# Where operand tiles start in SBUF: one attention-plus-MLP kernel with its weight blocks, x tiles and g tiles moved by multiples of 16 bytes

## The chip, the cores and the metric

The kernel runs on one core of one Trainium2 chip. The metric is the device time of one execution in microseconds (us). The kernel before has a median of 676.92 us in two runs (676.63 and 677.21).

## What is computed

Sliding-window attention with four sink positions, and then a two-layer MLP over the same tokens. The reference, cut to its core:

```python
# q, k, v: (4, 8, 768, 64); n_sink 4, window 128
scores = q @ k^T / sqrt(64)
keep = is_sink | in_window          # 4 first positions, or the last 128
a = exp(where(keep, scores, -1e9) - max); a = a / (sum(a) + 1e-9)
x = (a @ v) -> (3072, 512)          # heads side by side
h = x @ w_in                        # 512 -> 2048
g = max(h, 0) + alpha * min(h, 0)
out = g @ w_out                     # 2048 -> 512
```

## The kernel before

**Tiling.** The 3072 tokens are worked on in 12 chunks of 256 (`QC`). The 2048 hidden columns are worked on in 16 blocks of 128 (`f` = 0 to 15). For each chunk the attention part makes x, transposed, as four pieces of 128 x 256 (`kt` = 0 to 3). Each pair of chunk and block is one *round* of the MLP.

**Two parts per number.** The weights arrive as 64-bit floats and are turned on the chip into a high and a low 32-bit part. x and g are split likewise (`xh`, `xl`, `gh`, `gl`). Every product is the sum of three: high by high, high by low, low by high.

**One round.** `gemm1` (line 895) runs twelve matmuls of 256 columns into one PSUM bank: for each `kt`, `xh` and then `xl` stream past the high part of the w_in block, and then `xh` past the low part. So x is the moving operand, and a 128 x 128 slice of the weight block is loaded into the array. ScalarE and VectorE then make g (lines 899 and 900) and split it (901 and 902). `gemm2` runs two rounds later (`LAG` = 2) and is six matmuls of 512 columns: here the w_out half of the block is the moving operand and halves of `gh` or `gl` are loaded into the array (lines 932 and 933 with `gh`, line 930 with `gl`). TensorE loads the weights of the next matmul while one is running (rows PEld in the profile), and each of the eighteen matmuls of a round has its own load.

```python
for n, (part, rhs) in enumerate(((0, x1), (0, x2), (1, x1))):
    nc.tensor.matmul(h(), fin.at[:, 0, part, ks], rhs.at[:, kt], ...)   # L895
...
nc.tensor.matmul(o2[j].at, gh.at[:, js], fin.at[:, 1, 0], ...)          # L932
nc.tensor.matmul(o2[j].at, gh.at[:, js], fin.at[:, 1, 1], ...)          # L933
nc.tensor.matmul(o2[j].at, gl.at[:, js], fin.at[:, 1, 0], ...)          # L930
```

**Weights stay in SBUF.** Each block `f` has 8 KB of each partition in the pool `const`, under the tag `w0` to `w15`. The DMA (line 373) lands the raw 64-bit block there, ACT and DVE convert it by way of `wa` (lines 383 to 405), and the result is written over the raw block. This happens once, in about the first 113 us; after that all sixteen blocks lie still and are only read. The blocks 14 and 15 also serve, before their weights arrive, as room for the first heads (`lent`).

**What sets the order.** A planner (`Plan`) draws up one order of all operations before anything is built, from costs written down in the code. It knows of operations and of how many tiles of a kind there are, not of addresses. Each kind of tile (`xh`, `xl`: 2 each; `gh`, `gl`: `LAG + 1` = 3 each) is handed out in turn. Within a chunk the attention of the next chunk is spread over the first twelve rounds; the last chunk has none to carry, so that its sixteen rounds hold matmuls of `gemm1` and `gemm2` and almost nothing else. Since `gemm2` lags by two, the first two `gemm2` of a chunk's rounds are those of blocks 14 and 15 of the chunk before.

**Addresses.** Tiles of a pool lie one behind the other, each starting at a multiple of 32 bytes of the partition. `const` holds, before the weight blocks, only small tiles, and block 14 comes first of the blocks. Counted modulo 128 bytes, the kernel before has its operands here: all weight blocks at 32, but block 14 at 64; `xh` and `xl` at 96; `gh` and `gl` at 32 (a tile of 64 bytes named `gap` ahead of them is used by nothing). The inner slices of all these tiles start at multiples of 512 bytes, so that every slice has the place of its tile.

Of the kernel before, what the change touches and what calls it, by code (L numbers as in the profile page):

```python
# [9 lines left out]
F32 = mybir.dt.float32  # L10
F32R = mybir.dt.float32r
# [4 lines left out]
I32 = mybir.dt.int32  # L16
# [3 lines left out]
P = 128  # L20
B, H, S, D = 4, 8, 768, 64
DM, DF = 512, 2048
NS = 4
WIN = 2 * P + NS
QC = 2 * P
# [4 lines left out]
KT = DM // P  # L30
LAG = 2
# [47 lines left out]
class Plan:  # L79
# [20 lines left out]
    def held(self, tile_):  # L100
        v = Value(None)
        v.at = tile_
        return v

    def op(self, engine, cost, run, reads=(), writes=(), tail=0.09, mode=None, nbytes=0, other=None, locks=False):
        o = Op(engine, cost, tail, run, self.rank if engine == "PE" else None)
        o.ways = {engine: (cost, run)}
        if other:
            o.ways[other[0]] = other[1:]
        o.born = self.rank  # L110
        if engine == "PE":
            self.rank += 1
        o.mode, o.nbytes, o.index = mode, nbytes, len(self.ops)
        seen = []
        for group, writing in ((reads, False), (writes, True)):
            for x in group:
                v, key = x if isinstance(x, tuple) else (x, None)
                if v not in seen:
                    seen.append(v)
                keys = [k for k in set(v.wrote) | set(v.read) if key is None or k is None or k == key]  # L120
                for k in keys:
                    o.before.update(v.wrote.get(k, ()))
                    if writing:
                        o.before.update(v.read.get(k, ()))
                if writing:
                    for k in keys:
                        if key is None or k == key:
                            v.wrote.pop(k, None)
                            v.read.pop(k, None)
                    v.wrote.setdefault(key, []).append(o)  # L130
                else:
                    v.read.setdefault(key, []).append(o)
        for v in seen:
            v.left += 1
        o.values = seen
        o.takes = [v for v in seen if v.kind]
        o.locks = locks
        self.ops.append(o)
        return o
# [144 lines left out]
def dve(n, fast=False):  # L284
    return 0.07 + (0.52e-3 if fast else 1.04e-3) * n


def cast(n, psum=False):
    return (0.045 if psum else 0.092) + 0.84e-3 * n


def act(n, psum=False):
    return (0.153 if psum else 0.135) + 0.84e-3 * n
# [28 lines left out]
def program(ctx, tc, qk, pairs, vp, vq, vs, w, par, out):  # L322
    nc = tc.nc
    const = ctx.enter_context(tc.tile_pool(name="const", bufs=1))
    fast = ctx.enter_context(ExitStack())
    pool = fast.enter_context(tc.tile_pool(name="main", bufs=1))
    psum = ctx.enter_context(tc.tile_pool(name="psum", bufs=1, space=bass.MemoryType.PSUM))
    plan = Plan(tc)
# [6 lines left out]
    def several(name, n, shape, dtype):  # L335
        plan.kind(name, [pool.tile(shape, dtype, name=f"{name}{i}") for i in range(n)])

    scratch = ctx.enter_context(tc.tile_pool(name="scratch", bufs=1, space=bass.MemoryType.DRAM))
    plan.kind("swap", [scratch.tile([4, P, P], F32, name=f"swap{i}") for i in range(2)])
    plan.kind("turns", [scratch.tile([4, P, 2 * 32], F32, name=f"turns{i}") for i in range(2)])  # L340
# [13 lines left out]
    several("sinkT", 1, [P, QC], F32R)  # L354
    several("vs", 1, [P, DM], F32R)
    several("ob", 2, [P, DM], F32)
    several("xh", 2, [P, KT, QC], F32R)
    several("xl", 2, [P, KT, QC], F32R)
    several("g", 2, [P, QC], F32)
    pool.tile([P, 16], F32, name="gap")  # L360
    several("gh", LAG + 1, [P, QC], F32R)
    several("gl", LAG + 1, [P, QC], F32R)

    size = const.tile([P, NF], F32, name="size")
    sizes = held(size)
    raws, fins = {}, {}

    def load_weights(f, engine="ACT"):
        raw = raws[f] = held(None)

        def run():
            raw.at = const.tile([P, 2 * DM, 2], I32, tag=f"w{f}", name="wraw")
            (nc.sync if engine == "SP" else nc.scalar).dma_start(
                raw.at.rearrange("p (i x) w -> p i (x w)", i=2), w[f].bitcast(I32).rearrange("i p x -> p i x"))
        return op(engine, ISSUE if engine == "SP" else 0.12, run, writes=[raw] + lent.get(f, []), nbytes=8 * P * 2 * DM)

    def convert_weights(f):
        raw, fin, wa = raws[f], held(None), val("wa")
        fins[f] = fin
        n = 2 * DM  # L380
        low, high = lambda: raw.at[:, :, 0], lambda: raw.at[:, :, 1]
        wf = lambda: wa.at.bitcast(F32).rearrange("p (i x) -> p i x", i=2)
        first = op("ACT", act(n) + 0.09, lambda: nc.scalar.activation(  # L383
            wa.at.bitcast(F32), high().bitcast(F32), AF.Abs, scale=REBIAS, accum_out=size[:, f:f + 1]),
            reads=[raw], writes=[wa, (sizes, f)])
        if f < LATER:
            op("DVE", dve(n, True), lambda: nc.vector.tensor_scalar(wa.at, wa.at, 3, None, op0=ALU.logical_shift_left), writes=[wa])
            op("DVE", dve(n), lambda: nc.vector.scalar_tensor_tensor(
                wa.at, low(), 29, wa.at, op0=ALU.logical_shift_right, op1=ALU.bitwise_or), reads=[raw], writes=[wa])
        else:  # L390
            three = held(None)
            op("ACT", act(n), lambda: nc.scalar.activation(
                low(), raw.at.bitcast(U16).rearrange("p x (w s) -> p x w s", s=2)[:, :, 0, 1], AF.Copy, scale=2.0 ** -13, bias=-0.5 + 2.0 ** -14),
                reads=[raw], writes=[three])
            op("DVE", dve(n), lambda: nc.vector.scalar_tensor_tensor(  # L395
                wa.at, wa.at, 3, low(), op0=ALU.logical_shift_left, op1=ALU.bitwise_or), reads=[raw, three], writes=[wa])
        op("DVE", dve(n), lambda: nc.vector.scalar_tensor_tensor(  # L397
            wa.at, high(), -0x80000000, wa.at, op0=ALU.bitwise_and, op1=ALU.bitwise_or), reads=[raw], writes=[wa])

        def high_part(engine):  # L400
            fin.at = const.tile([P, 2, 2, DM], F32R, tag=f"w{f}", name=f"w{f}")
            (nc.scalar.copy if engine == "ACT" else nc.vector.tensor_copy)(fin.at[:, :, 0], wf())
        op("ACT", cast(n), lambda: high_part("ACT"), reads=[wa], writes=[(fin, 0), raw],
           other=("DVE", dve(n, True), lambda: high_part("DVE")))
        op("DVE", dve(n), lambda: nc.vector.tensor_tensor(  # L405
            fin.at[:, :, 1], wf(), fin.at[:, :, 0].bitcast(F32), ALU.subtract), reads=[wa, (fin, 0)], writes=[(fin, 1)])
        return first
# [82 lines left out]
    then(lambda: load_head(0, 2))  # L490
    then(lambda: load_head(0, 4))
    then(lambda: load_weights(0, "SP"))
    then(lambda: vs_prep(0))
    then(lambda: load_head(0, 6))
    then(lambda: load_v(0, 0))
    then(lambda: load_v(0, 2))
    for f in range(1, FIRST):
        then(lambda: load_weights(f, "SP"))
        if f == 2:
            then(lambda: load_head(1, 0))  # L500
            then(lambda: load_head(1, 2))
# [36 lines left out]
    for i, m in ((0, P), (1, P), (1, 0), (2, P), (2, 0)):  # L538
        o = m + NS if m else m
# [8 lines left out]
    xh, xl, prep, comb, sink, ptile_, sums, rinv, nms, wt = {}, {}, {}, {}, {}, {}, {}, {}, {}, {}  # L548
# [460 lines left out]
    def fetch(upto):  # L1009
        nonlocal nload  # L1010
        while nload < min(NF, upto):
            o = load_weights(nload)
            if nload - AHEAD in begun:
                plan.order_after(o, begun[nload - AHEAD])
            nload += 1
# [89 lines left out]
    with tc.If(bad != 0):  # L1105
# [3 lines left out]
        with tc.For_i(0, B, 1) as b:  # L1109
            for cc in range(CPB):  # L1110
                x = general(nc, gen, ptile, cc, b, qk5, vp5, nsink, window, ident)
# [167 lines left out]
```

## Time and profile before

| what | value |
|---|---|
| median of two runs | 676.92 us |
| span of the profiled execution (first to last instruction) | 674.6 us |
| matmuls / weight loads in the profile | 4534 / 4534 |
| of these in `gemm1` / `gemm2` | 2304 / 1152 in the program |
| VectorE, ScalarE busy | 525.4 us, 397.9 us |
| mean DMA rate | 126 GB/s |

The profiled execution's own span is 674.6 us, 2.3 us under the median of the runs; what lies ahead of the first and behind the last instruction is not in the span.

How to read it: the matmuls overlap in the records, since the end that the profile gives to a matmul is modelled. What a matmul takes of the time of TensorE is the distance from its start to the start of the next one. In a stretch without waits the given duration is that distance plus 0.163 us, so that a mean duration of 282 ns stands for 119 ns from start to start, and one of 390 ns for 227 ns. PEld rows are weight loads, which run beside the matmuls.

### The profile page before, as it was taken

Reading aid. Unit: us, or ns where it says so; the run is one execution under the profiler, and the core shown is the slowest. Engines: PE = TensorE matmul, PEld = TensorE weight load, DVE = VectorE, ACT = ScalarE, POOL = GpSimd, SP = SyncE. Lnnn points to the kernel's source line nnn. Section 1 sums busy time; section 2 is a strip of 40 time slices with the busy share of each in tenths; the row PEclk is TensorE's granted clock in tenths of the full one; section 3 lists DMA queues with packets and bytes.
Section 4 is the critical chain, followed back from the end, with each engine's and each line's share of the span. In section 5 each row is a group of like instructions: output and inputs, shape, how many; then the busy total and the mean of one; then the engine's idle time right before and its main releaser. Section 6 shows DMA issues by size and latency. Waiting matters only on the chain.

```text
span 674.6 us, 13245 instructions
## 1 busy us (share of the span) xinstructions
PE 661.7 (98%) x4534; PEld 579.3 (86%) x4534; DVE 525.4 (78%) x1750; ACT 397.9 (59%) x1066; POOL 35.0 (5%) x115
## 2 busy tenths in 40 slices
PE   9989999999999999999999999999999999999996
PEld 4667898888989989989988988988998988998995
DVE  6999999968967977986986985995995994994331
ACT  5999888827537627736636635744744753853332
POOL 2110000001000000010000000010000000000000
PEclk9999999999999999999999999999999999999999
DMA  8684641424343443443434433542542542420000
GB/s 319 218 307 155 241 162 48 119 76 154 119 126 107 128 143 106 139 136 86 142 117 119 142 118 89 159 141 59 174 129 72 162 131 87 142 94 17 32 2 35
DMA packets 58683, 85.19 MB, mean 126 GB/s; under 512 B 9072, under 2 KB 35056, under 8 KB 58608
## 3 DMA queue, kind: packets, MB, share of 16 engines
q1 hardware_dynamic: 55056, 71.17, 34.5%
q10 hardware_dynamic: 3552, 13.11, 5.3%
q8 instruction: 37, 0.61, 0.4%
q14 instruction: 38, 0.31, 0.2%
HBM read 67.22 MB, written 17.04 MB: 125 GB/s over the span
## 4 chain that ended last, share of the span: by engine, by line
PE 81%; DVE 11%; ACT 5%; issue 2%; POOL 0%; ACTq 0%; POOLq 0%
PE bank L895 35%; PE bank L932 11%; PE bank L933 11%; PE bank L930 11%; PE bank L787 3%; PE bank L599 3%; PE bank L598 3%; DVE wa L397 2%; PE bank L876 2%; DVE w L405 2%; ACT pt L615 1%; DVE wa L395 1%; ACT wa L383 1%; PE bank L1087 1%; DVE g L900 1%
## 5 line engine op out<-in xcount | busy, mean ns | idle before, releaser
L895 PE MATMUL bank<-xh,w 128*128 128x256 f32 x1536 | 307.5, 282 | 0.5 <-DVE g L900 0.3
L895 PEld LDWEIGHTS bank<-xh,w 128*128 128x128 f32 x1536 | 250.0, 189 | 9.3 <-DVE g L900 3.4
L895 PE MATMUL bank<-xl,w 128*128 128x256 f32 x768 | 214.9, 280 | 0.1
L899 ACT ACTIVATE g<-bank,param 128x256 f32<-128x256 f32 x192 | 90.7, 473 | 115.8 <-PE bank L895 110.1
L932 PE MATMUL bank<-w,gh 128*128 128x512 f32 x382 | 150.6, 394 | 0.2
L933 PE MATMUL bank<-w,gh 128*128 128x512 f32 x382 | 149.4, 391 | 0.0
L895 PEld LDWEIGHTS bank<-xl,w 128*128 128x128 f32 x768 | 144.4, 188 | 4.2 <-DVE xl L809 0.3
L615 ACT ACTIVATE pt<-pt,nm 128x260 f32<-128x260 f32 (+1 forms) x192 | 94.5, 493 | 54.0 <-DVE nm L611 53.5
L900 DVE TENSOR_TENSOR g<-bank,g 128x256 f32<-128x256 f32 x192 | 79.7, 419 | 50.7 <-ACT g L899 49.5
L930 PE MATMUL bank<-w,gl 128*128 128x512 f32 x382 | 118.9, 392 | 0.0
L901 ACT CAST gh<-g 128x256 fp32r<-128x256 f32 x192 | 76.9, 404 | 60.9 <-DVE g L900 60.7
L902 DVE TENSOR_TENSOR gl<-g,gh 128x256 fp32r<-128x256 f32 x192 | 80.4, 423 | 26.4 <-ACT gh L901 23.0
L611 DVE CUSTOM_DVE_ANT_0 pt<-bank,masks 128x260 f32<-128x260 f32 (+1 forms) x192 | 74.9, 400 | 19.4 <-PE bank L599 15.8
L930 PEld LDWEIGHTS bank<-w,gl 128*128 128x128 f32 x382 | 70.6, 188 | 14.9 <-issue 0.7
L932 PEld LDWEIGHTS bank<-w,gh 128*128 128x128 f32 x382 | 71.7, 188 | 9.7 <-ACT gh L901 1.0
L933 PEld LDWEIGHTS bank<-w,gh 128*128 128x128 f32 x382 | 71.8, 188 | 8.1
L564 DVE TENSOR_TENSOR kq<-stage,kq 64x392 fp32r<-64x392 f32 x80 | 45.3, 567 | 2.7
L660 POOL TENSOR_TENSOR sink<-pt,ri 128x8 f32<-128x8 f32 x80 | 20.8, 263 | 503.9 <-DVE ri L645 386.1
L598 PE MATMUL bank<-kq 128*128 128x260 f32 (+1 forms) x160 | 44.5, 278 | 1.3 <-DVE nm L611 1.2
L599 PE MATMUL bank<-kq 128*128 128x260 f32 (+1 forms) x160 | 45.1, 282 | 0.0
L656 DVE CUSTOM_DVE_ANT_0 comb<-pt,ri 128x128 f32<-128x128 f32 x136 | 43.1, 343 | 0.4
L562 ACT CAST kq<-stage 128x392 fp32r<-128x392 f32 x80 | 40.9, 512 | 0.6 <-PE bank L599 0.2
(130 smaller groups left out, 685.5 us busy)
## 6 DMA issues: line engine op xcount, KB each, us to landing
stage<-qk SPq DMA_DIRECT2D x80, 324.0 KB, 2.9
wraw<-w ACTq DMA_DIRECT2D x12, 1024.0 KB, 5.6
swap<-comb SPq DMA_DIRECT2D x36, 256.0 KB, 2.0
comb<-swap SPq DMA_DIRECT2D x36, 256.0 KB, 3.1
v<-vq SPq DMA_DIRECT2D x36, 192.0 KB, 2.7
out_dram<-ob SPq DMA_DIRECT2D x22, 256.0 KB, 3.6
wraw<-w SPq DMA_DIRECT2D x4, 1024.0 KB, 11.0
v<-vp SPq DMA_DIRECT2D x8, 192.0 KB, 7.3
```

Of the source, the lines that this page charges most:

```text
L598: nc.tensor.matmul(s[:, w0], qh()[:, qs], ks()[:, kw], start=True, stop=False)
L599: nc.tensor.matmul(s[:, w0], ql()[:, qs], ks()[:, kw], start=False, stop=True)
L611: op("DVE", dve(n), lambda: nc.vector.tensor_tensor_reduce(out=pt.at[:, u, w0], in0=s.at[:, w0], in1=masks[:, i, w0], scale=-0.125, scalar ...
L615: op("ACT", exp(n), lambda: nc.scalar.activation(pt.at[:, u, w0], pt.at[:, u, w0], AF.Exp, bias=nm.at[:, h, u:u + 1], scale=-1.0, accum_ou ...
L895: nc.tensor.matmul(h(), fin.at[:, 0, part, ks], rhs.at[:, kt], start=(kt == 0 and n == 0), stop=(kt == KT - 1 and n == 2))
L899: op("ACT", act(QC, True), lambda: nc.scalar.activation(g.at, h(), AF.Copy, scale=alt[:, f:f + 1]), reads=[bk, known("param")], writes=[g])
L900: op("DVE", dve(QC), lambda: nc.vector.tensor_tensor(g.at, h(), g.at, ALU.max), reads=[bk], writes=[g])
L901: op("ACT", cast(QC), lambda: nc.scalar.copy(gh.at, g.at), reads=[g], writes=[gh])
L902: op("DVE", dve(QC), lambda: nc.vector.tensor_tensor(gl.at, g.at, gh.at.bitcast(F32), ALU.subtract), reads=[g, gh], writes=[gl])
L930: nc.tensor.matmul(o2[j].at, gl.at[:, js], fin.at[:, 1, 0], start=False, stop=(f == NF - 1))
L932: nc.tensor.matmul(o2[j].at, gh.at[:, js], fin.at[:, 1, 0], start=(f == 0), stop=False)
L933: nc.tensor.matmul(o2[j].at, gh.at[:, js], fin.at[:, 1, 1], start=False, stop=False)
```

## The change

The instructions, their order, their engines and their waits are the same. What changes is where three groups of tiles start in SBUF:

- Each weight block has 8224 bytes in place of 8192 (`4 * DM + 8` words), so that the start moves on by 32 bytes modulo 128 from one block to the next; and for `f` = 4 to 7 and 12 to 15 the block is used from 16 bytes behind the tile's start.
- `xh0` and `xl0` come first, then a tile of 8 bytes that takes 32, then `xh1` and `xl1`.
- `gh` and `gl` are laid out in three sets, with a tile of 40 bytes (it takes 64) behind each; the former `gap` of 64 bytes is gone.

```diff
+    def apart(name, n, kinds, shape, words):
+        sets = []
+        for i in range(n):
+            sets.append([pool.tile(shape, F32R, name=f"{k}{i}") for k in kinds])
+            pool.tile([P, words], F32, name=f"gap{name}{i}")
+        for k, tiles in zip(kinds, zip(*sets)):
+            plan.kind(k, list(tiles))
...
-    several("xh", 2, [P, KT, QC], F32R)
-    several("xl", 2, [P, KT, QC], F32R)
+    apart("x", 2, ("xh", "xl"), [P, KT, QC], 2)
     several("g", 2, [P, QC], F32)
-    pool.tile([P, 16], F32, name="gap")
-    several("gh", LAG + 1, [P, QC], F32R)
-    several("gl", LAG + 1, [P, QC], F32R)
+    apart("g", LAG + 1, ("gh", "gl"), [P, QC], 10)
...
+    def placed(f, dtype, name):
+        o = f // 4 % 2 * 4
+        return const.tile([P, 4 * DM + 8], dtype, tag=f"w{f}", name=name)[:, o:o + 4 * DM]
...
-            raw.at = const.tile([P, 2 * DM, 2], I32, tag=f"w{f}", name="wraw")
+            raw.at = placed(f, I32, "wraw").rearrange("p (x w) -> p x w", w=2)
...
-            fin.at = const.tile([P, 2, 2, DM], F32R, tag=f"w{f}", name=f"w{f}")
+            fin.at = placed(f, F32R, f"w{f}").rearrange("p (i n x) -> p i n x", i=2, n=2)
```

Where the operands start, in bytes modulo 128, from the addresses that the two programs are built with:

| operand | before | after |
|---|---|---|
| w0 to w3 | 32, 32, 32, 32 | 96, 32, 64, 96 |
| w4 to w7 | 32, 32, 32, 32 | 16, 48, 80, 112 |
| w8 to w11 | 32, 32, 32, 32 | 0, 32, 64, 96 |
| w12 to w15 | 32, 32, 64, 32 | 16, 16, 80, 80 |
| xh0, xl0 / xh1, xl1 | 96 / 96 | 96 / 0 |
| gh0, gl0 / gh1, gl1 / gh2, gl2 | 32 / 32 / 32 | 32 / 96 / 32 |

All other tiles keep their size. Those that lie behind a moved one move along with it by multiples of 32 bytes, the constants `ident`, `param`, `tri` and `masks` among them.

## The prediction

> **What bounds the kernel now.** I read the page's table of engines first, then the chain of work that ended last, then the busy time in three stretches, and then the groups of TensorE inside the long stretch.
>
> ```profile
> PE 661.7 (98%) x4534; PEld 579.3 (86%) x4534; DVE 525.4 (78%) x1750; ACT 397.9 (59%) x1066; POOL 35.0 (5%) x115
> ...
> PE 81%; DVE 11%; ACT 5%; issue 2%; POOL 0%; ACTq 0%; POOLq 0%
> ```
>
> ```profile
> 0.00:115.00 115.00, 109.42 (x704) 83.60 (x704) 106.33 (x243) 97.67 (x219) 11.24 (x34) 1.00 0.59 211
> 115.00:665.00 550.00, 548.45 (x3818) 492.92 (x3817) 418.21 (x1506) 298.39 (x845) 23.72 (x81) 1.00 0.37 110
> 665.00:674.60 9.60, 3.82 (x17) 2.78 (x15) 0.85 (x2) 1.81 (x4) 0.00 (x0) 0.89 0.17 61
> ```
>
> The columns of the stretches are the time, then busy time and count of PE, PEld, DVE, ACT and POOL, the granted clock (1.00 is full; 0.89 in the tail), the DMA share and GB/s. The reader is to see two regimes. Up to 115 us VectorE is full (106.33 of 115) with converting the weights. From 115 to 665 us TensorE is busy 548.45 of 550.00 us at a full clock, with 418.21 us of VectorE beside it. So in 550 of the 674.6 us nothing but the distance from one matmul to the next counts, and a change that adds no instruction can move the time only through that distance (or by making the first stretch longer).
>
> What that distance is now, from the groups of this long stretch (columns: count, busy us, mean ns of one, idle before):
>
> ```profile
> L895 PE MATMUL bank<-xh,w 128*128 128x256 f32 x1343 | 268.3, 282 | 0.5 <-DVE g L900 0.3
> L895 PE MATMUL bank<-xl,w 128*128 128x256 f32 x671 | 187.7, 280 | 0.1
> L932 PE MATMUL bank<-w,gh 128*128 128x512 f32 x336 | 132.1, 393 | 0.0
> L933 PE MATMUL bank<-w,gh 128*128 128x512 f32 x335 | 131.0, 391 | 0.0
> L930 PE MATMUL bank<-w,gl 128*128 128x512 f32 x334 | 103.8, 392 | 0.0
> ```
>
> With 163 ns taken off each modelled duration, `gemm1` has (1343 x 282 + 671 x 280) / 2014 - 163 = 118.3 ns a matmul, 1.42 us a round of twelve; `gemm2` has 392 - 163 = 229 ns, 1.374 us a round of six. The stretch holds 2014 / 12 = 168 rounds. These 168 x 2.79 = 469 us are the bulk of the 550.
>
> **Does the place of a tile show in the trace before?** Once in each chunk it does, since block 14 lies at 64 and the other fifteen at 32. The last chunk carries no attention, so that its rounds can be laid side by side. Its start times, with the first matmul of each part:
>
> ```profile
> 621.35 0.28 PE L895 MATMUL bank<-xh,w 128*128 128x256 f32 x1
> ...
> 622.77 0.40 PE L932 MATMUL bank<-w,gh 128*128 128x512 f32 x1
> ...
> 624.17 0.28 PE L895 MATMUL bank<-xh,w 128*128 128x256 f32 x1
> ...
> 625.54 0.39 PE L932 MATMUL bank<-w,gh 128*128 128x512 f32 x1
> ...
> 626.91 0.28 PE L895 MATMUL bank<-xh,w 128*128 128x256 f32 x1
> ...
> 628.33 0.39 PE L932 MATMUL bank<-w,gh 128*128 128x512 f32 x1
> ...
> 629.69 0.28 PE L895 MATMUL bank<-xh,w 128*128 128x256 f32 x1
> ```
>
> The `gemm2` at 622.77 is that of block 14 (from the chunk before), at 625.54 of block 15, at 628.33 of block 0. They take 624.17 - 622.77 = 1.40, 1.37 and 1.36 us. So `gemm2` with the weight block 32 bytes off the place of `gh` costs 0.04 us more than with both at 32. The same in single matmuls, line 930 of block 14 (first row) and of block 0 (second):
>
> ```profile
> L930 PE MATMUL bank<-w,gl 128*128 128x512 f32 x2 | 0.6, 400 | 0.0
> ```
>
> ```profile
> L930 PE MATMUL bank<-w,gl 128*128 128x512 f32 x2 | 0.6, 389 | 0.0
> ```
>
> `gemm1` reads otherwise. With the same places (x at 96, block at 32) it takes 622.77 - 621.35 = 1.42 us for block 0, 1.37 for block 1 and 1.42 for block 2. So the same places allow two speeds, and what went before picks one. For block 14, at the end of the chunk:
>
> ```profile
> 657.51 0.28 PE L895 MATMUL bank<-xh,w 128*128 128x256 f32 x1
> ...
> 658.92 0.39 PE L932 MATMUL bank<-w,gh 128*128 128x512 f32 x1
> ...
> 660.29 0.28 PE L895 MATMUL bank<-xh,w 128*128 128x256 f32 x1
> ...
> 661.70 0.40 PE L932 MATMUL bank<-w,gh 128*128 128x512 f32 x1
> ```
>
> Block 13 (x and block 64 apart) takes 658.92 - 657.51 = 1.41 us, block 14 (32 apart) 661.70 - 660.29 = 1.41 us. Here the place does nothing.
>
> **The change, part by part.** Nothing is added or removed, no instruction moves in any queue, no wait is new.
>
> *`gemm2`.* Before, block and g stand at the same place in fifteen blocks of sixteen. After, g stands at 32 in two of its three sets and at 96 in one, and the sets go round. Two blocks (1, 9) match the 32 and three (0, 3, 11) the 96, so the two agree in 2/3 x 2/16 + 1/3 x 3/16 = 0.15 of the rounds. Of the 168 rounds 143 then disagree, against the 11 or so of block 14 now: 132 rounds more. The price of one is bounded by the rows above: 0.04 us by the undisturbed neighbours (1.40 against 1.36), and 1.40 - 1.374 = 0.026 us against the mean of all rounds, which pay for other things too. That is 132 x 0.026 = 3.4 to 132 x 0.04 = 5.3 us. A gain at other distances than 32 isn't excluded by any row; it is bounded below by 1.36 us in all rounds, -(1.374 - 1.36) x 168 = -2.4 us. I take 5 us, near the undisturbed pair.
>
> *`gemm1`.* Before, x and block stand 64 apart (32 for block 14); after, 16, 32, 48, 64 and so on, and 0. Nearest row: block 14, no difference. A mixture of places is already there in the attention, where the two `kq` tiles start at 96 and 0 and their slices add 0, 16 and 32 bytes:
>
> ```profile
> L599 PE MATMUL bank<-kq 128*128 128x260 f32 x130 | 36.8, 283 | 0.0
> ```
>
> 283 against the 280 of `xl` above is 3 ns more, of which four more columns are 4 x 117 / 256 = 1.8 ns. The rest, 1.2 ns on 2014 matmuls, is 2.4 us. The other way, if all rounds ran at the quick 1.37 us: 168 x 0.05 = -8.4 us. So -8.4 to +2.4 us; I take 0, since the row that has this very instruction at another place shows none.
>
> *The first stretch.* The conversions on VectorE set its end. They write and read blocks at 32 and, for block 14, at 64 without a difference:
>
> ```profile
> L405 DVE TENSOR_TENSOR w<-wa,w 128x1024 fp32r<-128x1024 f32 x16 | 19.5, 1221 | 0.8 <-ACT w L402 0.8
> ...
> L397 DVE SCALAR_TENSOR_TENSOR wa<-wraw,wa 128x1024 int32<-128x1024 int32 x16 | 19.5, 1216 | 0.1
> ```
>
> ```profile
> L405 DVE TENSOR_TENSOR w<-wa,w x16: 1215/1220/1227, 18.8 to 111.9; 128x1024 fp32r<-128x1024 f32 x16
> ```
>
> Shortest and longest of sixteen are 1215 and 1227 ns: price 0; if each of some 56 such instructions took the 12 ns more, 0.7 us. The loads of blocks 4 to 7 and 12 to 15 land 16 bytes off. The cover is the time from issue to first use, tightest for block 12:
>
> ```profile
> 78.15 0.37 ACTq L373 DMA_DIRECT2D wraw<-w  x1
> ...
> 85.00 1.15 ACT L383 ACTIVATE wa<-wraw 128x1024 f32<-128x1024 f32 x1
> ```
>
> ```profile
> wraw<-w ACTq DMA_DIRECT2D x12, 1024.0 KB, 5.6
> ```
>
> 6.85 us against a median of 5.6 to landing leaves 1.2 us. So a landing that is 20% longer costs nothing; one twice as long would cost 4.4 us here, and what is late next is the conversion on a full VectorE. Price 0.
>
> *Sum:* 5 + 0 + 0 = +5 us. The profiled execution's 674.6 us become 679.6; the runs' median stands 2.3 us above its span, so 676.9 + 5 = 682 us.
>
> **The rivals.** (1) *No effect.* The difference at block 14 comes from something else that returns once a chunk (it is the turn to a new chunk), and the place is read without cost: 677 us. Against it: block 15 has its turn right behind and is back at 1.37. The Trainium skill has this rival as a rule: "TensorE: Matmul & The Clock Gate", section "Step-by-step: what each phase is for", gives the array two independent SBUF read ports, so that loading the next weights takes nothing from the running matmul, and "SBUF — State Buffer", section "Who interferes with whom", says that PE and ACT never wait on anyone. By that rule the sum would be 0 and the time 677 us; the 400 against 389 ns of line 930 speak against it.
>
> (2) *Faster.* The two speeds of `gemm1` at equal places say that a lock between the running matmul and the load beside it decides. Broken by places that change each round, it may fall into the quick one: -8.4 - 2.4 = -10.8 us, 666 us. For it: block 1's 1.37 us came right behind block 14's odd place. Against it: the `gemm2` in front of it had paid 0.04 us, which is nearly all that was won.
>
> (3) *Slower than the forecast.* Most places are as bad as the worst pair seen, 400 against 389 ns, for `gemm2` throughout, and half as much (half the columns) for `gemm1`: 11 x 1008 + 5.5 x 2014 = 22 us, 699 us. It counts as slower, beyond 2% (13.5 us), from about 60% of that price on. Against it: block 14's `gemm1`.
>
> (4) *The loads.* Landings at 16-byte starts take twice as long: some 4 to 9 us of the first stretch, 681 to 686 us without the rest.
>
> **How the numbers follow.** A small loss (677.5 to 690.5 us): 0.53; its likeliest is 682. No effect: 0.12. Faster, 664 to 676: 0.18, of which 0.04 beyond 2%. Worse than 690.5: 0.15. The loads: 0.02, inside the same bounds as the small loss. The range from 668 to 694 leaves out some 0.07 below and 0.12 above. A change of about 2% is what a measurement of this kernel can tell from none; 2% are 663.4 and 690.5 us. So faster 0.04, slower 0.15, same 0.81.
>
> **What would show it.** In the profile after: line 930, 932 and 933 at means of some 395 to 398 ns instead of 391 to 393, line 895 at 280 to 282 still, the same counts, and a first stretch that still ends near 115 us. In the last chunk, `gemm2` at 1.40 us where block and g differ and 1.36 where they agree (block 9). Wrong, if line 895 moves by more than 2 ns in the mean, if the distance of blocks and g doesn't sort the rounds, or if ScalarE's first reads of the raw blocks begin to wait for DMA.

## The result and the profile after

The kernel after takes 682.63 us (median of 2 runs, 682.52 to 682.75) against 676.92 us: a ratio of 1.0085, 95% interval [1.0055, 1.0114]. That is slower, by 5.7 us, and within 2%. The forecast was 682 us. The total came out as forecast, in part by luck: of its two big terms one was too large and the other, put at nothing, was not nothing.

First the page of the kernel after, the table of engines and the loads of the weights, and then the busy time in the two long stretches:

```profile
PE 668.2 (98%) x4534; PEld 584.6 (86%) x4534; DVE 526.7 (77%) x1750; ACT 398.9 (59%) x1066; POOL 34.5 (5%) x115
...
wraw<-w ACTq DMA_DIRECT2D x12, 1024.0 KB, 5.4
```

```profile
0.00:115.00 115.00, 109.59 (x698) 84.83 (x699) 106.24 (x241) 97.11 (x217) 10.64 (x33) 0.99 0.58 211
115.00:665.00 550.00, 548.54 (x3783) 491.33 (x3782) 417.89 (x1505) 298.00 (x843) 23.84 (x82) 1.00 0.36 110
```

The span grew from 674.6 to 680.8 us. The first stretch is as full of VectorE as before (106.24 against 106.33 us) and the twelve loads of ScalarE's queue land as fast (5.4 against 5.6 us). In the same 550 us TensorE got through 3783 matmuls in place of 3818, at a full clock, and as busy as before. Every matmul takes a little longer. By groups of the long stretch:

```profile
L904 PE MATMUL bank<-xh,w 128*128 128x256 f32 x1327 | 268.3, 283 | 0.4 <-DVE g L909 0.2
L904 PE MATMUL bank<-xl,w 128*128 128x256 f32 x664 | 186.6, 281 | 0.1
L941 PE MATMUL bank<-w,gh 128*128 128x512 f32 x330 | 130.5, 395 | 0.0
L942 PE MATMUL bank<-w,gh 128*128 128x512 f32 x330 | 130.2, 394 | 0.0
L939 PE MATMUL bank<-w,gl 128*128 128x512 f32 x331 | 104.1, 395 | 0.0
```

(Line 904 is the former 895, lines 941, 942 and 939 the former 932, 933 and 930.) `gemm2` went up by 2 to 3 ns a matmul, and `gemm1`, which was to stay, by 1 ns. These means are rounded to a nanosecond, which on 3000 matmuls is worth some us; adding up the distances from start to start in both traces, from 115 us to the end, gives it more closely:

```
start to next start, us in all      before    after
gemm1 (xh and xl past w)             238.9    242.7   +3.8
gemm2 (w past gh and gl)             236.0    238.6   +2.6
attention (kq, sinkT, wa, comb)       76.7     76.7    0.0
```

Five more matmuls of `gemm1` fall into this stretch after (2016 against 2011), which is 0.6 of its 3.8 us; so `gemm1` grew by 3.2 and `gemm2` by 2.6 us, together 5.8 us of the 6.2 us of the span, and what is left falls to the first stretch, whose conversions end 0.7 us later (113.8 against 113.1 us; in `e8_w14_in_step` below, which as a whole takes as long as before, they end at 113.6 us).

What the last chunk shows, in starts of the parts (`gemm1` of block 0, `gemm2` of block 14, `gemm1` of block 1, `gemm2` of block 15, and so on, as in the prediction), and further on `gemm2` of block 9:

```profile
626.97 0.28 PE L904 MATMUL bank<-xh,w 128*128 128x256 f32 x1
...
628.39 0.40 PE L941 MATMUL bank<-w,gh 128*128 128x512 f32 x1
...
629.79 0.28 PE L904 MATMUL bank<-xh,w 128*128 128x256 f32 x1
...
631.23 0.40 PE L941 MATMUL bank<-w,gh 128*128 128x512 f32 x1
...
632.64 0.28 PE L904 MATMUL bank<-xh,w 128*128 128x256 f32 x1
...
634.06 0.39 PE L941 MATMUL bank<-w,gh 128*128 128x512 f32 x1
...
635.45 0.28 PE L904 MATMUL bank<-xh,w 128*128 128x256 f32 x1
...
659.52 0.39 PE L941 MATMUL bank<-w,gh 128*128 128x512 f32 x1
...
660.91 0.28 PE L904 MATMUL bank<-xh,w 128*128 128x256 f32 x1
```

`gemm2` takes 1.40, 1.41 and 1.39 us here. Block 9 stands at 32 like its g (both at 160 modulo 256) and was to be back at 1.36; it takes 660.91 - 659.52 = 1.39 us. The three rounds of this chunk whose block and g agree modulo 128 (blocks 1, 9 and 11) take 1.387, 1.387 and 1.399 us by unrounded starts, the others between 1.380 and 1.412: the distance doesn't sort them. `gemm1` takes 1.42, 1.44 and 1.42 us. The rounds are no longer alike, and no `gemm2` of these is as quick as the 1.36 us that was usual before.

### The profile page after: what moved, and what is told of

The parts are those of the page before. It is cut to its first block, busy times and chain, and to the rows that moved or that the text cites. A ratio compares the mean times of both kernels' runs of the same rounds, so it can differ in the third digit from the quotient of the medians.

```text
span 680.8 us, 13245 instructions
## 1 busy us (share of the span) xinstructions
PE 668.2 (98%) x4534; PEld 584.6 (86%) x4534; DVE 526.7 (77%) x1750; ACT 398.9 (59%) x1066; POOL 34.5 (5%) x115
## 4 chain that ended last, share of the span: by engine, by line
PE 88%; DVE 4%; ACT 4%; DMA 1%; issue 1%; POOL 0%; SPq 0%; ACTq 0%; POOLq 0%
PE bank L904 39%; PE bank L941 13%; PE bank L942 12%; PE bank L939 12%; PE bank L796 3%; PE bank L608 3%; PE bank L607 3%; PE bank L885 2%; ACT pt L624 1%; DMA wraw<-w 1%; ACT wa L392 1%; DVE wa L406 1%; PE bank L869 1%; ACT w L411 1%; DVE pt L620 0%
## 5 line engine op out<-in xcount | busy, mean ns | idle before, releaser
L904 PE MATMUL bank<-xh,w 128*128 128x256 f32 x1536 | 312.4, 284 | 0.4 <-DVE g L909 0.2
L908 ACT ACTIVATE g<-bank,param 128x256 f32<-128x256 f32 x192 | 90.7, 473 | 122.6 <-PE bank L904 121.3
## 6 DMA issues: line engine op xcount, KB each, us to landing
wraw<-w SPq DMA_DIRECT2D x4, 1024.0 KB, 11.9
```

What stands on the lines that cost most here:

```text
L908: op("ACT", act(QC, True), lambda: nc.scalar.activation(g.at, h(), AF.Copy, scale=alt[:, f:f + 1]), reads=[bk, known("param")], writes=[g])
```

## The experiments

Two theories were set against each other. *D*: the distance between the two operands of a matmul, the streaming and the loaded one, sets its price, pair by pair. *L*: the train of matmuls and loads falls into a repeating beat when all rounds have the same places, the beat's level depends on the places, and places that change from round to round break it. Times of each run are compared with runs of the kernel before on the same chip (676.8 to 677.0 us).

**One half of the change alone.** `e1_w_only` moves the blocks only, `e2_xg_only` x and g only, to the kernel after's places modulo 128 (the tiles are made 128 bytes longer, so that their places modulo 256 differ from those of the kernel after).

```diff
...
+    WORDS = (16, 0, 8, 16, 28, 4, 12, 20, 24, 0, 8, 16, 28, 28, 4, 12)
+    def placed(f, dtype, name):
+        return const.tile([P, 4 * DM + 32], dtype, tag=f"w{f}", name=name)[:, WORDS[f]:WORDS[f] + 4 * DM]
...
```

```diff
+    def shifted(name, words, n, view, **k):
+        plan.kind(name, [pool.tile([P, n + 32], F32R, name=f"{name}{i}")[:, o:o + n].rearrange(view, **k) for i, o in enumerate(words)])
...
-    several("xh", 2, [P, KT, QC], F32R)
-    several("xl", 2, [P, KT, QC], F32R)
+    shifted("xh", (0, 8), KT * QC, "p (k x) -> p k x", k=KT)
+    shifted("xl", (0, 8), KT * QC, "p (k x) -> p k x", k=KT)
...
-    several("gh", LAG + 1, [P, QC], F32R)
-    several("gl", LAG + 1, [P, QC], F32R)
+    shifted("gh", (0, 16, 0), QC, "p x -> p x")
+    shifted("gl", (0, 16, 0), QC, "p x -> p x")
```

> Only the weight blocks are moved, to the places of the kernel after; x stays at 96, g at 32. Theory D (the distance of the two operands of a matmul sets its price, and only gemm2 pays): 147 of 168 rounds have block and g apart, 136 more than before, at 0.026 to 0.04 us: +3.5 to +5.4 us, 680.5 to 682.5 us, gemm1's mean durations unchanged at 282 and 280 ns, and in the last chunk gemm2 of blocks 1 and 9 back at 1.36 us. Theory L (one relation for all rounds lets the train of matmuls fall into a repeating beat, and places that change from round to round break it, for all matmuls): some +4 to +6 us as well, but gemm1's means go up by 1 to 2 ns, and blocks 1 and 9 cost as much as the others in gemm2, about 1.39 us.

> Only x (96 / 0) and g (32 / 96 / 32) are moved, as in the kernel after; the blocks stay at 32, block 14 at 64. Theory D: a third of the gemm2 rounds, 56, are at a distance of 64, at 0.026 to 0.04 us: +1.5 to +2.2 us, about 679 us; gemm1 as before; in the last chunk two gemm2 of three at 1.36 us and the third at about 1.40. Theory L: x changes once a chunk and g in every third round, so the beat is broken three times less often than with the blocks moved: +1 to +4 us, and the gemm1 that follows an odd gemm2 changes too.

Measured: 682.43 us, ratio 1.0076 [1.0059, 1.0093], and 682.22 us, 1.0074 [1.0057, 1.0091]. Either half costs nearly the whole, so the halves don't add. With the blocks moved, `gemm1` is up as well (283 and 281 ns by the same groups) and `gemm2` of blocks 1 and 9, which stand with their g modulo 256 too, takes 1.38 us, nearer to L's 1.39 than to D's 1.36. With x and g moved, D had 679 us and L at most 4 us more than before; both are passed. All of `gemm2`, not a third, sits at 1.38 to 1.405 us, and from block 2 to block 11 the third whose g is 64 bytes off is the quickest (1.38 us), where D had it as the slowest.

**All blocks at one place.** `e3_w14_as_others` puts all blocks at 32 modulo 128, `e4_all_w_64` all at 64, with blocks 8320 bytes apart in place of 8192 (`WORDS` all 0 but 24 for block 14; or all 8 but 0 for block 14).

> Block 14 is put at 32 like the other fifteen: one relation for the whole kernel. Theory D: 11 rounds win 0.026 to 0.04 us, -0.3 to -0.4 us, 676.5 us. Theory L: the same, and in the last chunk all gemm2 at 1.36 us, block 15's too, and gemm1 at 1.41 to 1.42 throughout, so that block 1's 1.37 us is gone. No effect of places at all: 676.9 us and gemm2 of block 14 still 1.40 us.

> All sixteen blocks at 64, block 14's place, x at 96 and g at 32: one relation again, but 32 bytes apart in gemm2. Theory D: every gemm2 costs what block 14's does, 1.40 us: 157 rounds more at 0.026 to 0.04 us, +4.1 to +6.3 us, 681 to 683 us. Theory L: with one relation the beat holds; its level is that of this relation, equal in all gemm2 of the last chunk to 0.01 us, and may lie on either side of 1.40: 670 to 684 us.

Measured: 678.71 us, 1.0027 [1.0013, 1.004], and 681.85 us, 1.0074 [1.0057, 1.009]. The first was to be a little quicker than before and is slower. A round of its last chunk (`gemm1` of block 4, `gemm2` of block 2):

```profile
634.42 0.28 PE L900 MATMUL bank<-xh,w 128*128 128x256 f32 x1
...
635.83 0.40 PE L937 MATMUL bank<-w,gh 128*128 128x512 f32 x1
...
637.22 0.28 PE L900 MATMUL bank<-xh,w 128*128 128x256 f32 x1
```

`gemm2` takes 1.39 us, not 1.36, though modulo 128 all is as before. What differs is the step of the blocks, 8192 + 128, so that modulo 256 every other block stands 128 bytes off. If 128 bytes were the period that counts, this would change nothing. The same round of `e4_all_w_64`, whose `gemm2` rounds take 1.385 to 1.400 us, near block 14's 1.40:

```profile
636.70 0.28 PE L900 MATMUL bank<-xh,w 128*128 128x256 f32 x1
...
638.11 0.39 PE L937 MATMUL bank<-w,gh 128*128 128x512 f32 x1
...
639.50 0.28 PE L900 MATMUL bank<-xh,w 128*128 128x256 f32 x1
```

**One distance at a time, strides as before.** The next four keep tiles and blocks as long as they were and move whole groups with a pad (in e6 and e7 what lies behind g is put back, modulo 256, by a second one).

```diff
# e5_x_at_0: x 160 bytes on
+    pool.tile([P, 40], F32, name="gapx")
     several("xh", 2, [P, KT, QC], F32R)
...
-    pool.tile([P, 16], F32, name="gap")
+    pool.tile([P, 40], F32, name="gap")
# e6_no_gap: g 64 bytes back
-    pool.tile([P, 16], F32, name="gap")
# e7_g_128_on: g 128 bytes on
-    pool.tile([P, 16], F32, name="gap")
+    pool.tile([P, 48], F32, name="gap")
# e8_w14_in_step: all blocks but 14, x and g 160 bytes on
     idle = const.tile([P, 2], BF16, name="idle")
+    const.tile([P, 40], F32, name="gapw")
```

> Only x is moved, all four tiles by 160 bytes (from 224 to 128 modulo 256), so that x and block are 96 apart in every gemm1 but block 14's; blocks and g stay. Theory D for gemm1 (the distance of x and block sets the level; the runs so far show 119.8 ns a matmul at 96 and 116.1 at 64 or 192): gemm1's means go up by 3 to 4 ns, 2016 x 15/16 x 3.7 = +7 us, 684 us, gemm2 at 229 ns as before. The forecast's step (the place does nothing in gemm1): 677 us. Theory L (only mixing places costs): 677 us, since all rounds are alike, with perhaps another level of the beat.

682.94 us, 1.0075 [1.0047, 1.0104]: the step of the forecast that put `gemm1` at nothing is refuted by moving x alone (g lies 256 bytes further on, at the same place modulo 256). Two rounds in a row, `gemm1`, `gemm2`, `gemm1`, `gemm2`:

```profile
636.96 0.28 PE L896 MATMUL bank<-xh,w 128*128 128x256 f32 x1
...
638.41 0.39 PE L933 MATMUL bank<-w,gh 128*128 128x512 f32 x1
...
639.80 0.28 PE L896 MATMUL bank<-xh,w 128*128 128x256 f32 x1
...
641.23 0.40 PE L933 MATMUL bank<-w,gh 128*128 128x512 f32 x1
...
642.60 0.28 PE L896 MATMUL bank<-xh,w 128*128 128x256 f32 x1
```

`gemm1` takes 1.44 and 1.43 us (1.443 and 1.427 by unrounded starts) where it was 1.41, the way that D says. But `gemm2`, whose operands keep their places modulo 256, takes 1.39 and 1.37 in turn where it was 1.36: the beat now repeats after two rounds, and `gemm2` pays along with `gemm1`, as L says. From 115 us on the mean distance grew from 118.8 to 121.3 ns in `gemm1`, some 4.9 us where D had 7, and from 231.6 to 232.9 ns in `gemm2`, some 1.3 us. Neither theory is enough alone.

> The 64 bytes of gap ahead of gh and gl are taken out (and put behind), so that g stands 64 bytes from its block modulo 128 in every gemm2; blocks and x stay. Theory D for gemm2: 231 to 233 ns a matmul in place of 229, 1008 x 3 = +3 us, 680 us, gemm1 as before. Theory L: all rounds are alike, so the beat holds at some level of its own, and gemm2's six take the same time in all sixteen rounds of the last chunk to 0.005 us; anywhere from 674 to 683 us.

> gh and gl are moved by 128 bytes, so that modulo 128 nothing has changed and modulo 256 everything has for gemm2. If places count modulo 128 alone: 677 us and gemm2 of the last chunk at 1.36 us as before. If they count modulo 256 or more, as the run with block 14 moved (blocks 8320 bytes apart) suggests: gemm2 at 231 to 232 ns, 1.385 us, +2.5 us, 679.5 us, gemm1 as before.

677.33 us, 1.0006 [0.9992, 1.002]: no difference that can be told. 678.25 us, 1.0017 [1.0004, 1.003]: slightly slower. First a round without the gap, then one with g 128 bytes on:

```profile
633.70 0.28 PE L895 MATMUL bank<-xh,w 128*128 128x256 f32 x1
...
635.08 0.39 PE L932 MATMUL bank<-w,gh 128*128 128x512 f32 x1
...
636.46 0.28 PE L895 MATMUL bank<-xh,w 128*128 128x256 f32 x1
```

```profile
634.94 0.28 PE L896 MATMUL bank<-xh,w 128*128 128x256 f32 x1
...
636.35 0.39 PE L933 MATMUL bank<-w,gh 128*128 128x512 f32 x1
...
637.73 0.28 PE L896 MATMUL bank<-xh,w 128*128 128x256 f32 x1
```

Without the gap both parts take 1.38 us (1.386 and 1.374 by unrounded starts): `gemm2` is slower and `gemm1`, whose places are untouched, quicker. D's 680 us was missed. After block 8, ahead of which a lone transposition stands (one matmul with `ident`), the same kernel runs at 1.41 and 1.39 us to the end of the chunk's alike rounds: one set of places, two levels. So L missed too, which had all sixteen `gemm2` equal to 0.005 us. With g 128 bytes on, `gemm2` is 1.37 (1.373) in place of 1.36 in the alike rounds, less than the 1.385 expected: modulo 128 nothing has changed, so that the period seems to be more than 128.

> Block 14 in step with the others modulo 1024, with the blocks 8192 bytes apart as before (all behind it, x and g included, move on by 160 bytes together, so that their distances stay). Theory D: 11 rounds of block 14 win 0.026 to 0.04 us: -0.3 to -0.4 us, 676.5 us; in the last chunk gemm2 at 1.36 us and gemm1 at 1.414 us throughout. If the absolute place counts and not the distance, gemm2 or gemm1 take another level in all rounds, by 0.01 us or more.

676.29 us, 0.9993 [0.9976, 1.0009]: not to be told from no change, and in line with the 0.3 to 0.4 us expected. From block 15's `gemm2` on all rounds but the two at the transposition read like this one, 1.41 and 1.36 us:

```profile
632.58 0.28 PE L895 MATMUL bank<-xh,w 128*128 128x256 f32 x1
...
633.99 0.39 PE L932 MATMUL bank<-w,gh 128*128 128x512 f32 x1
...
635.35 0.28 PE L895 MATMUL bank<-xh,w 128*128 128x256 f32 x1
```

Blocks, x and g have all moved by 160 bytes together, and the level stayed.

**Towards a quicker one.** `e9_no_gap_in_step` joins e6 and e8. `e10_g_112` and `e12_x_48` move g or x alone by 16-byte steps, with block 14 in step. `e11_all_16_on` moves blocks, x and g together by 16 bytes, with 256 bytes added to each tile so that the places modulo 256 are equal in a kind.

```diff
# e11_all_16_on
...
+        plan.kind(name, [pool.tile([P, n + 64], F32R, name=f"{name}{i}")[:, o:o + n].rearrange(view, **k) for i in range(count)])
...
+    shifted("xh", 2, KT * QC, 4, "p (k x) -> p k x", k=KT)
+    shifted("xl", 2, KT * QC, 4, "p (k x) -> p k x", k=KT)
...
+    shifted("gh", LAG + 1, QC, 4, "p x -> p x")
+    shifted("gl", LAG + 1, QC, 4, "p x -> p x")
...
+        o = 4 if f != NF - 2 else 28
+        return const.tile([P, 4 * DM + 64], dtype, tag=f"w{f}", name=name)[:, o:o + 4 * DM]
# e10_g_112: gh and gl with 36 for 4; e12_x_48: xh and xl with 28 for 4
```

> Meant to beat both: block 14 in step with the others (modulo 256, as in e8) and no gap ahead of gh and gl (as in e6), so that x stands 192 and the block 64 from its partner modulo 256. e6's last chunk had rounds of 1.386 + 1.374 = 2.760 us beside the 2.774 of before, until a disturbance took it to 1.413 + 1.393. Theory L (the beat that a round falls into decides): with block 14 out of the way the quicker beat lasts longer: 168 rounds at -0.005 to -0.014 us are -0.8 to -2.4 us, 674.5 to 676 us. Theory D (distance alone): e6's +0.5 us less 0.4 us, 677 us.

> All blocks in step, x as before (192 from the block), g at 112 from its block modulo 256, a 16-byte step. In the mixtures this distance had the lowest mean of gemm2, 229.4 ns. Theory D for gemm2, by distances (0: 228, 64: 230.8, 128: 231.8, 32 and 160: 233.5): 229 to 231 ns, +1 to +3 us on e8, 677 to 679 us. If a start off the 32-byte grid costs by itself: over 234 ns, above 681 us.

677.73 us, 1.0015 [1.0006, 1.0024], and 678.36 us, 1.0017 [1.0008, 1.0027]. The first missed: it runs the first half of its last chunk at 1.41 and 1.39 us and falls into the quicker beat (1.386 and 1.374) only behind the transposition, and there stays. Here is one of the quicker rounds, and then two rounds of `e10_g_112`:

```profile
652.60 0.28 PE L896 MATMUL bank<-xh,w 128*128 128x256 f32 x1
...
653.99 0.39 PE L933 MATMUL bank<-w,gh 128*128 128x512 f32 x1
...
655.36 0.28 PE L896 MATMUL bank<-xh,w 128*128 128x256 f32 x1
```

```profile
634.28 0.28 PE L898 MATMUL bank<-xh,w 128*128 128x256 f32 x1
...
635.70 0.39 PE L935 MATMUL bank<-w,gh 128*128 128x512 f32 x1
...
637.09 0.28 PE L898 MATMUL bank<-xh,w 128*128 128x256 f32 x1
...
638.46 0.40 PE L935 MATMUL bank<-w,gh 128*128 128x512 f32 x1
...
639.87 0.28 PE L898 MATMUL bank<-xh,w 128*128 128x256 f32 x1
```

By unrounded starts, `gemm1` of `e10_g_112` takes 1.413 and 1.373 us in turn with x and blocks as far apart as before, and `gemm2` 1.393 and 1.401: again a beat of two rounds. A start off the 32-byte grid didn't cost the 234 ns that would have spoken for it, but `gemm2` is slower than D's 229 to 231 ns as well (1.397 us a round in the mean, 232.8 ns).

> All blocks, x, gh and gl 16 bytes further on than before, block 14 in step, so that every distance in gemm1 and gemm2 is that of e8 and every start is off the 32-byte grid, the landings of the loads too. Theory D (only distances count): as e8, 676 to 677 us, gemm1 1.413 and gemm2 1.360 us in the last chunk, the conversions at an end near 113.6 us. If 16-byte starts cost by themselves, in TensorE's reads or in the DMA's writes: gemm1 or gemm2 above that in all rounds, or the first stretch longer, 678 us or more.

> All blocks in step, g as before (0 from the block), x 48 from its block modulo 256, a 16-byte step. The mixtures have two rounds at this distance, at 116.6 ns a matmul, and rounds at 176 (the same modulo 128) at 118.8. Theory D for gemm1 modulo 256: 116.6 in all rounds, +0.6 x 2016 = +1.2 us on e8, 677.5 us. By distance modulo 128 alone: 117 to 119 ns, +2 to +6 us, 678.5 to 682.5 us.

675.09 us, 0.997 [0.9955, 0.9985]: quicker than both kernels, and the best that was found. And 680.61 us, 1.0051 [1.0032, 1.0071]. A round of `e11_all_16_on`, and below it one of `e12_x_48`:

```profile
633.55 0.28 PE L902 MATMUL bank<-xh,w 128*128 128x256 f32 x1
...
634.91 0.39 PE L939 MATMUL bank<-w,gh 128*128 128x512 f32 x1
...
636.29 0.28 PE L902 MATMUL bank<-xh,w 128*128 128x256 f32 x1
```

```profile
636.44 0.28 PE L898 MATMUL bank<-xh,w 128*128 128x256 f32 x1
...
637.86 0.40 PE L935 MATMUL bank<-w,gh 128*128 128x512 f32 x1
...
639.23 0.28 PE L898 MATMUL bank<-xh,w 128*128 128x256 f32 x1
```

With all distances modulo 256 as in e8, e11 holds 1.36 us in every `gemm1` of the last chunk but the one at the transposition, and 1.38 in `gemm2`: 2.74 us a round in place of 2.77. So D, by distances modulo 256 alone, fails here. Its profiled execution was the longest of its five (677.05 us), and the gain doesn't show in that span (675.1 us against 674.6 before): the conversions began at 12.8 us in place of 11.2 and ended at 115.6 in place of 113.1. It shows in the distances from 115 us on: 117.2 ns in place of 118.8 in `gemm1` and 232.8 in place of 231.6 in `gemm2`, or some -3.2 and +1.2 us. In e12 x was to cost 116.6 ns a matmul by two rounds seen in a mixture; it takes 1.42 us a `gemm1`, 118.5 ns. Two rounds in a mixture don't foretell an unmixed kernel.

**A rival that a trace answers.** No run was made against the thought that TensorE's reads are held up by those of VectorE and ScalarE. The trace before answers it for `gemm1`. In block 0's `gemm1` (621.35 to 622.77 us) ScalarE works until 621.63 and VectorE until 622.08, and then neither to the end of this `gemm1`:

```profile
621.66 0.42 DVE L902 TENSOR_TENSOR gl<-g,gh 128x256 fp32r<-128x256 f32 x1 [0.47 <-ACT gh L901]
...
622.18 0.28 PE L895 MATMUL bank<-xl,w 128*128 128x256 f32 x1
...
622.53 0.28 PE L895 MATMUL bank<-xl,w 128*128 128x256 f32 x1
```

The matmuls stand 117 to 119 ns apart in both halves, so the slower level doesn't need the other engines' work. In block 1's `gemm1`, with the same places and VectorE at work from 624.43 to 624.86 us, the first two matmuls take 118 and 116 ns and the other ten 113 or 114, with VectorE at work or not. So the two levels are there matmul by matmul.

All runs side by side, from the start times of the last chunk (mean of `gemm1` without block 8 and of `gemm2` without block 5, which have the transposition in them, their sum, and the median time):

```
                     gemm1   gemm2   round   time
e11_all_16_on        1.360   1.380   2.740   675.1
e8_w14_in_step       1.411   1.362   2.773   676.3
before               1.410   1.368   2.778   676.9
e9_no_gap_in_step    1.401   1.384   2.784   677.7
e6_no_gap            1.397   1.388   2.785   677.3
e7_g_128_on          1.410   1.379   2.789   678.3
e10_g_112            1.394   1.397   2.791   678.4
e3_w14_as_others     1.407   1.384   2.792   678.7
e12_x_48             1.422   1.378   2.799   680.6
e4_all_w_64          1.408   1.396   2.804   681.9
e1_w_only            1.418   1.391   2.809   682.4
e5_x_at_0            1.429   1.385   2.813   682.9
after                1.423   1.394   2.817   682.6
e2_xg_only           1.433   1.396   2.829   682.2
```

The round of the last chunk sorts the times of the fourteen kernels, but for one pair in the middle and the last four, which lie within 0.7 us. So the time goes with the distance from matmul to matmul, whichever tiles were moved.

## Why the forecast came out as it did, point by point

- *The bound.* Right: from 115 us on the distance between matmuls is all that counts; the matmuls of attention took 76.7 us before and after.
- *`gemm2`, +5 us.* The direction was right. The size measured is +2.6 us, under the lower bound of 3.4. The price of 0.026 to 0.04 us a round was near (in the last chunk the mean went from 1.368 to 1.394 us), but what was counted, the rounds whose places differ, is not what pays: agreeing rounds pay too (block 9: 1.39 us). Modulo 256, which e3 and e7 speak for, block and g agree in 0.06 of the rounds, not in 0.15. The trace before held a warning: `gemm2` of block 12, which stands where its g stands, takes 1.39 us there, right behind block 14's `gemm1`.

```profile
661.70 0.40 PE L932 MATMUL bank<-w,gh 128*128 128x512 f32 x1
...
663.08 0.28 PE L895 MATMUL bank<-xh,w 128*128 128x256 f32 x1
```

- *`gemm1`, 0, at most +2.4 us.* This step failed: +3.2 us. It rested on block 14, 32 bytes from x, taken for any place. The runs show that places differ: x at 96 bytes from its block takes `gemm1` from 1.41 to 1.43 and 1.44 us, and the kernel is 0.75% slower (e5). One row at one other place bounds nothing for the rest. The `kq` row of the attention, a mixture of places, came nearer with its 2.4 us and was used only as an end of the range; that it measures the same thing isn't shown.
- *The first stretch, 0.* Right to within 0.7 us: 106.24 us of VectorE in 115, loads at 5.4 us. In e11, with all landings off the 32-byte grid, the twelve loads take no longer either (5.2 us by its page). The four first loads, on the other queue, take 11.9 us in the median (12.1 in e11) against 11.0 before, and 11.7 in e8, whose landings are on that grid.
- *The sum.* 5 + 0 was to be 5; it was 2.6 + 3.2 = 5.8 from 115 us on, 6.2 in the span and 5.7 in the medians. Two errors of opposite sign cancelled: that the total came within 1 us was luck, and the likeliest case was right for a partly wrong reason.
- *The rivals.* No effect is excluded by the interval. The faster one did not come; its thought, that a beat decides and can be quick, fits e6, e9 and e11, but what locks isn't shown. The slower one needed 60% of its price and got 26% (5.7 of 22 us). The loads did nothing. Behind the first rival stood a rule of the Trainium skill ("TensorE: Matmul & The Clock Gate", section "Step-by-step: what each phase is for": two independent read ports, so that a load takes nothing from the running matmul). What was drawn from it, no effect of the places, did not come: moving x alone by 160 bytes cost 6 us, ratio 1.0075. Whether the running matmul loses that to the load beside it, no run here shows.
- *The marks.* `gemm2` at 394 to 395 ns was foretold as 395 to 398. `gemm1` did stay within 2 ns in the mean, though its 283 ns lies outside the 280 to 282 foretold: 1 ns on 2016 matmuls is 2 us, so that this mark was too coarse for the term it watched. ScalarE's first reads of the raw blocks waited for a load once, for 0.2 us, as they do in e8. That the distance of block and g would sort the rounds of the last chunk was wrong, and was named beforehand as what would make the prediction wrong.

What stays open: what in the reads makes the levels. The runs show that they depend on the places (e5) and on what went before (e6 on two levels). That 128 bytes are not the period rests on e3 and e7, two small differences with one profiled execution each; since equal places can run at two levels, they speak for it without settling it. In e11 blocks and g step by 256 bytes modulo 512 from tile to tile and its rounds are alike all the same, so that no run asks for a period over 256. e11 also lengthened the tiles by 256 bytes, so that its gain isn't shown to be due to the 16 bytes alone.

## What to carry to other kernels

When TensorE is full and everything else is hidden, the placing of tiles in SBUF is a knob of about a per cent: here from 675.1 to 682.9 us with the same instructions in the same order. Give all tiles of a kind the same place modulo 256: the mixtures e1 to e4 and the kernel after took 678.7 to 682.6 us, and the one kernel that was quicker than before had no mixture. The same place alone is no guarantee, since e5, with a single block out of step, was the slowest of all. So try a few common shifts, judged by the distance between starts in a stretch without other matmuls, which shows a difference of 0.005 to 0.008 us in a round where the whole time leaves it unclear (e8, e6). Don't take the price of one place for that of another.

## What the runs showed of the hardware that was not expected

- Equal instructions on equal places run at two levels that hold for many rounds: twelve 256-column matmuls of `gemm1` take 1.386 us in some rounds of e6 and 1.413 in others, and the change comes at a lone transposition (from quick to slow in e6, from slow to quick in e9). Before, block 1 alone took 1.37 us and its neighbours 1.41.
- The beat can span two rounds: `gemm1` takes 1.44 and 1.43 us in turn in e5, 1.41 and 1.37 in e10.
- Moving g by 128 bytes changes `gemm2` from 1.360 to 1.373 us (e7); moving blocks, x and g together by 160 bytes leaves the levels as they were (e8); everything by 16 bytes, with longer tiles, changes both parts by 0.02 to 0.05 us (e11).
